# Expert-layer tiles cut along the batches, the left-over rows in short units of 128, and x transposed 128 rows at a time

## The chip, the cores and the metric

The kernel runs on one core of one Trainium2 chip. The metric is the device time of the whole program in microseconds, median of three runs.

## The reference

Decayed causal attention over 8 batches of 8 heads, 576 positions of width 64, and then a two-layer expert block ("moe") on the 4608 rows of 512 values that come out, with 2048 hidden columns. Rows are the positions of a batch, one batch after the other.

```python
# per head of a batch
scores = scale * np.matmul(q, k.transpose(0, 1, 3, 2))
cum = np.cumsum(np.log(np.clip(f, 0.0001, 1.0)), axis=-1)
scores = np.where(causal, -1000000000.0, scores + cum[..., :, None] - cum[..., None, :])
attn = softmax(scores)                     # rows over their sum + 1e-9
x = np.matmul(attn, v)                     # heads side by side: 4608 x 512
# two layers
h = x @ w_in                               # 512 -> 2048
g = h * np.clip(h + 3.0, 0.0, 6.0) / 6.0
out = g @ w_out                            # 2048 -> 512
```

## The kernel before, in words

**Attention.** The heads are worked off one after the other: four pairs "A" and eight heads "B" for batch 0 (in two parts), then 56 whole heads "F" for batches 1 to 7. For an F head, `rows` (from line 591) makes the scores on TensorE in two halves (`pn`, lines 608 and 611), takes the row maxima on VectorE while it copies (`pp`, line 619), the exponentials on ScalarE (631), splits the result into a high and a low half-precision part in `ring` (ScalarE 645, VectorE 648, GpSimd 642, 654 and 659), and transposes that by DMA into `pT` (line 666, two a head). `av` multiplies it with v (`pav`, lines 691 to 696) and divides by the row sums into `xf` and its two halves `xhl`, [128, 5 chunks, 2 halves, 128 columns of a head pair]. In F heads chunk 0 holds the batch's first 64 positions and chunks 1 to 4 hold 128 each; in A and B heads chunks 0 to 3 hold 128 and chunk 4 the last 64.

**v.** `load_v(b)` loads a batch's v into the one buffer `vst` with three DMAs: two small ones (line 359) and the large one (360). `v_split` (lines 396 and 397) turns a head pair's part into half-precision v; `vst` may only be overwritten when the last pair of a batch is split. `v_scale` takes the greatest value of the new v on VectorE (`vm`, line 365) and makes the batch's scale from it.

**x.** When a head pair is done, `x_move` (line 736) transposes `xhl` by DMA into `xT`, from which the first layer reads. SP issues every DMA of the kernel, in the order of its queue.

**Two layers.** The 4608 rows are cut into nine tiles of 512 rows, whatever the batch: tile t holds the last 64 t rows of batch t - 1 and the first 512 - 64 t of batch t, and tiles 7 and 8 both need batch 7. For each of 16 groups of 128 hidden columns `h_unit` (769) makes 12 products of 512 columns into one PSUM bank (`ph`, lines 778 to 780: high x high, high x low, low x high, over four blocks of 128 inputs), ScalarE applies the first half of the activation with the batch's scale, once for each batch in the tile (788), VectorE the second (791), and ScalarE (792) and VectorE (793) split the result into `gT`. `out_unit` (796) then makes 128 rows of output from 48 products of 512 columns (`po`, lines 800 to 802), scales them (811) and stores them (812). Banks come from three buffers in turn.

**What sets the order.** The tiles are generators in a queue (`queue`, `fill`): between the steps of a head, as many product groups are taken from the queue as a rate says. The rate is fixed for batches 0 and 1, and from batch 2 on (`even`) spreads what is queued over the heads of a batch, so that a tile of batch b is worked off during batch b + 1. `done` queues tile b when batch b's x has been moved, and tiles 7 and 8 at the end. Below that, a list scheduler fixes each engine's final order when the program is built, by priorities and its own cost table; on the chip every engine goes through its list in order.

Of the kernel before, what the change touches and what calls it, by code (L numbers as in the profile page):

```python
# [20 lines left out]
def kernel(  # L21
# [23 lines left out]
    NCC = DM // P  # L45
    NFC = DFF // P
    TT = 512
# [70 lines left out]
    def init_qk(i, eng):  # L118
# [14 lines left out]
    w1 = [cpool.tile([P, NCC, DFF], F16, name=f"w1{i}") for i in range(2)]  # L133
    w2 = cpool.tile([P, NFC + 1, 2, DM], F16, name="w2")
    gT = cpool.tile([P, 2, NFC, TT], F16, name="gT")
    xT = [cpool.tile([P, NCC, 2, TT // P, 2, 64], F16, name=f"xT{i}") for i in range(3)]

    v0 = [
        v16.bitcast(F32).rearrange("p n c j e -> p (n c j e)")[:, 0:3 * VR],
        xT[2].bitcast(F32).rearrange("p a h c l t -> p (a h c l t)")[:, 0:2 * VR],  # L140
    ]
    v0 = [t.rearrange("p (c e) -> p c e", e=VR) for t in v0]

# [6 lines left out]
    NG = 4  # L150
# [49 lines left out]
    def scol(c):  # L200
        return SC[:, c:c + 1]
# [534 lines left out]
    def x_move(v):  # L736

        kind, n = VH[v]
        g = n if kind == "A" else n // 2
        b, cc = divmod(g, NPAIR)  # L740
        xhl = xpair[g][1]
        c0, c1 = {"A": (0, CA), "B": (CA, NCH), "F": (0, NCH)}[kind]

        if kind == "F":
            runs = [(0, 0, 1, 0), (0, 1, NCH, 1), (64, 1, NCH, 2)]
        else:
            runs = [(r * 64, c0, min(c1, NCH - r), r + 2 * c0) for r in range(2)]
        for r, c, last, u in runs:
            while c < last:
                t, q = divmod(S // 64 * b + u, TT // 64)  # L750
                k = min(last - c, (TT // 64 - q + 1) // 2)
                nc.sync.dma_start_transpose(  # L752
                    xT[t % 3][:, cc, q % 2, q // 2:q // 2 + k].rearrange("p c a t -> p (c a) t"),
                    xhl[r:r + 64, c:c + k].rearrange("p c a e -> p (c a e)"),
                )
                c += k
                u += 2 * k


    turn = [0]  # L760
# [1 line left out]
    def mm_tile(name, three):  # L762

        turn[0] += 1
        if three and turn[0] % 3 == 0:
            return ps_t.tile([P, TT], F32, tag="tr", name=name)
        return ps_m.tile([P, TT], F32, tag="mm", name=name)

    def h_unit(t, fc, c0, c1):
        x = xT[t % 3]  # L770
        nw = c1 - c0
        ph = mm_tile(f"ph_{t}_{fc}_{c0}", t > 0 or c0 > 0)[:, :nw]
        fs_ = slice(fc * P, (fc + 1) * P)
        for cc in range(NCC):
            xh, xl = (
                x[:, cc, :, c0 // P:c1 // P, hl].rearrange("p h c t -> p c h t") for hl in range(2)
            )
            nc.tensor.matmul(ph, w1[0][:, cc, fs_], xh, start=(cc == 0), stop=False)  # L778
            nc.tensor.matmul(ph, w1[0][:, cc, fs_], xl, start=False, stop=False)  # L779
            nc.tensor.matmul(ph, w1[1][:, cc, fs_], xh, start=False, stop=(cc == NCC - 1))  # L780
            if cc == 1 and nw == TT:
                yield H_COST
        r = p2.tile([P, TT], F32, tag="rt", name=f"r_{t}_{fc}_{c0}", bufs=3)[:, :nw]
        segs = [(0, nw, min(t, B - 1))]
        if 0 < t < B:
            segs = [(0, 64 * t, t - 1), (64 * t, TT, t)]
        for a, e, b in segs:
            nc.scalar.activation(  # L788
                r[:, a:e], ph[:, a:e], AF.Relu, bias=bias_r, scale=scol(A1 + NG * b + fc * NG // NFC)
            )  # L790
        nc.vector.scalar_tensor_tensor(r, r, 6.0 * CG, ph, op0=ALU.min, op1=ALU.mult)  # L791
        nc.scalar.copy(gT[:, 0, fc, c0:c1], r)  # L792
        nc.vector.tensor_tensor(gT[:, 1, fc, c0:c1], r, gT[:, 0, fc, c0:c1], op=ALU.subtract)  # L793
        yield H_COST

    def out_unit(t, s):
        po = mm_tile(f"po_{t}_{s}", t > 0 or s * P >= QA)
# [7 lines left out]
        g = t * 4 + s  # L805
        b = (g * P) // S
        col = UO + b
        if (g * P + P - 1) // S != b:
            col = UX + b + 1
        o = p2.tile([P, DM], F32, tag="o", name=f"o_{t}_{s}")  # L810
        nc.scalar.activation(o, po, AF.Copy, scale=scol(col))
        nc.sync.dma_start(out[g * P:(g + 1) * P, :], o)
        yield 2.0 - H_COST

    def moe_tile(t, c0=0, c1=TT):
        for fc in range(NFC):
            j, new = divmod(fc, NFC // NG)
            if new == 0 and t < B and c0 == 0:
# [7 lines left out]
        if t < B and c0 == 0:  # L826
            moe_scale_out(t)
        for s in range(c0 // P, c1 // P):
            yield from out_unit(t, s)


    dec = decay()
# [48 lines left out]
    def queue(unit, columns):  # L881
        units.append(unit)
        left[0] += TILE * columns / TT
# [22 lines left out]
    def one(*a):  # L906
        yield from moe_tile(*a)

    def done(v):
        kind, n = VH[v]  # L910
        if kind == "A":
            if n == NPAIR - 1:
                queue(one(0, 0, QA), QA)
            return
        b, h = divmod(n, H)
        if h == H - 1:
            queue(one(b, QA if b == 0 else 0, TT), TT - QA if b == 0 else TT)
            if b == B - 1:
                queue(one(B), TT)

    prev = None
    pend_x = moved = None
# [115 lines left out]
```

## Time and profile before

| | |
|---|---|
| runs | 1094.17, 1095.14, 1095.26 us (median 1095.14) |
| profiled execution, first to last instruction | 1093.0 us |
| TensorE busy (products) | 1013.8 us, 93% |
| VectorE, ScalarE, GpSimd busy | 728.9, 609.7, 414.4 us |
| mean granted TensorE clock | 0.981 |
| x transposes on SP (line 752) | 148 |

A row of a group in the profile gives line, engine, operation, what it writes and reads, shapes and count, then the busy time, the mean of one in ns, and the engine's idle time just before these instructions with what ended it. A row of the waits gives the engine and line that waited, what released it, and the total, count and longest wait. A row of the chain or the timeline begins with its start and its duration in us. A q behind an engine's name stands for its sequencer, which waits and issues DMAs. Products overlap, so the pace of a stream of products is read from the difference of their starts.

### The profile page before, as it was taken

How to read it: one execution, taken by the hardware profiler on the slowest of the kernel's cores; microseconds unless marked ns; L12 is line 12 of the kernel's file. 1: busy time of each engine (PE TensorE's matmuls, PEld its weight loads, DVE VectorE, ACT ScalarE, POOL GpSimd, SP SyncE). 2: the span in 40 equal slices, each digit the busy share in tenths (PEclk: the TensorE clock that was granted, in tenths of full speed). 3: DMA queues.
4: the chain of work that ended last, by engine and by line, in shares of the span. 5: the costliest groups of instructions: out<-in, count | busy, mean ns of one | idle time of the engine just before them, and what ended most of it. 6: DMA issues, size and time to landing. Idle time of an engine off the chain costs nothing.

```text
span 1093.0 us, 20322 instructions
## 1 busy us (share of the span) xinstructions
PE 1013.8 (93%) x7074; PEld 576.3 (53%) x7074; DVE 728.9 (67%) x1903; ACT 609.7 (56%) x1285; POOL 414.4 (38%) x505
## 2 busy tenths in 40 slices
PE   2799977899999989998999889999999999999998
PEld 2568844755555545554555445555555554444443
DVE  7888889877887669756876588569856840520520
ACT  4786656756765557545754566458646831621520
POOL 8443465345545434444534335453555300000000
PEclk9999989999999989998999989999999999999999
DMA  8966447866767656566566755785566530000001
GB/s 251 283 196 211 119 101 131 182 139 137 169 136 155 144 138 130 108 145 155 108 121 129 170 105 116 146 185 104 116 136 145 98 77 29 1 5 34 1 1 39
DMA packets 261651, 133.74 MB, mean 122 GB/s; under 512 B 229445, under 2 KB 231037, under 8 KB 261549
## 3 DMA queue, kind: packets, MB, share of 16 engines
q1 hardware_dynamic: 261548, 132.45, 54.0%
q8 instruction: 56, 0.92, 0.4%
q14 instruction: 47, 0.38, 0.1%
HBM read 47.93 MB, written 9.73 MB: 53 GB/s over the span
## 4 chain that ended last, share of the span: by engine, by line
PE 59%; DMA 6%; DVE 4%; issue 3%; SPq 3%; ACT 3%; POOL 2%; POOLq 0%; DVEq 0%; ACTq 0%
PE po L800 9%; PE po L802 9%; PE po L801 9%; PE ph L778 8%; PE ph L779 8%; PE ph L780 8%; DMA pT<-ring 3%; PE pn L611 3%; PE pn L608 3%; DMA vst<-in_vS_dram 2%; SPq L752 2%; DVE pp L619 1%; ACT pp L631 1%; PE pav L695 1%; PE pav L696 1%
## 5 line engine op out<-in xcount | busy, mean ns | idle before, releaser
L778 PE MATMUL ph<-xT,w 128*128 128x512 f16 (+1 forms) x640 | 229.2, 364 | 19.6 <-DVE r L791 19.4
L779 PE MATMUL ph<-xT,w 128*128 128x512 f16 (+1 forms) x640 | 228.5, 363 | 0.0
L780 PE MATMUL ph<-xT,w 128*128 128x512 f16 (+1 forms) x640 | 228.2, 362 | 0.0
L801 PE MATMUL po<-w,gT 128*128 128x512 f16 x576 | 214.3, 381 | 7.3 <-DVE w L294 7.3
L800 PE MATMUL po<-w,gT 128*128 128x512 f16 x576 | 212.1, 381 | 3.0 <-ACT w L283 2.2
L802 PE MATMUL po<-w,gT 128*128 128x512 f16 x576 | 214.1, 381 | 0.0
L631 ACT ACTIVATE pp<-pp,nb 128x192 f32<-128x192 f32 x280 | 138.8, 553 | 128.2 <-DVE nb L625 127.9
L648 DVE TENSOR_TENSOR ring<-pp,ring 128x128 f16<-128x128 f32 (+2 forms) x216 | 135.0, 635 | 70.1 <-ACT ring L645 69.2
L791 DVE SCALAR_TENSOR_TENSOR r<-r,ph 128x512 f32<-128x512 f32 (+1 forms) x160 | 99.9, 626 | 104.6 <-ACT r L788 104.4
L788 ACT ACTIVATE r<-ph,bias_r,SC 128x256 f32<-128x256 f32 (+7 forms) x272 | 144.1, 571 | 37.2 <-PE ph L780 33.3
L458 POOL TENSOR_TENSOR T<-ST,T 64x576 fp32r<-64x576 f32 (+1 forms) x68 | 100.6, 1480 | 153.5 <-DMA T<-TK 149.6
L792 ACT CAST gT<-r 128x512 f16<-128x512 f32 (+1 forms) x160 | 91.9, 575 | 89.6 <-DVE r L791 89.5
L619 DVE CUSTOM_DVE_ANT_0 pp<-pn,W 128x192 f32<-128x192 f32 x280 | 123.3, 482 | 26.1 <-PE pn L611 19.8
L608 PE MATMUL pn<-TK,TQ 68*128 68x192 f32 x336 | 127.0, 390 | 5.6 <-issue 4.0
L793 DVE TENSOR_TENSOR gT<-r,gT 128x512 f16<-128x512 f32 (+1 forms) x160 | 110.4, 693 | 29.2 <-ACT gT L792 28.5
L611 PE MATMUL pn<-T,T 128*128 128x192 f32 x336 | 116.2, 375 | 0.4 <-POOL T L458 0.4
L645 ACT CAST ring<-pp 128x192 f16<-128x192 f32 x280 | 115.7, 452 | 0.0
L455 POOL TENSOR_TENSOR T<-ST,TQ 64x576 fp32r<-64x576 f32 (+2 forms) x68 | 96.8, 1423 | 18.4 <-PE pn L611 8.7
L779 PEld LDWEIGHTS <-w 128*128 128x128 f16 x640 | 63.1, 99 | 75.2 <-issue 26.2
L780 PEld LDWEIGHTS <-w 128*128 128x128 f16 x640 | 63.2, 99 | 65.8 <-issue 9.2
L802 PEld LDWEIGHTS <-gT 128*128 128x128 f16 x576 | 56.5, 98 | 76.0 <-issue 14.6
L778 PEld LDWEIGHTS <-w 128*128 128x128 f16 x640 | 62.4, 99 | 59.1 <-issue 10.8
(136 smaller groups left out, 1713.6 us busy)
## 6 DMA issues: line engine op xcount, KB each, us to landing
ST<-in_qk_dram SPq DMA_DIRECT2D x64, 288.0 KB
T<-TK SPq DMA_DIRECT2D x64, 144.0 KB
out_dram<-o SPq DMA_DIRECT2D x36, 256.0 KB
ring<-in_w_out_dram SPq DMA_DIRECT2D x16, 512.0 KB
T<-TQ SPq DMA_DIRECT2D x56, 144.0 KB
vst<-in_vS_dram SPq DMA_DIRECT2D x7, 1040.0 KB
ring<-in_w_in_dram SPq DMA_DIRECT2D x9, 512.0 KB
w<-in_w_in_dram SPq DMA_DIRECT2D x7, 512.0 KB
```

The source lines that it names most:

```text
L608: nc.tensor.matmul(dst, TQ[i][0:D + 4, qs], TK[i][0:D + 4, a:e], start=True, stop=False)
L611: nc.tensor.matmul(dst, T7[j][:, qs], T1[j][:, a:e], start=False, stop=True)
L619: nc.vector.tensor_tensor_reduce(pp[:r, w:w + kw], pn[:r, o:o + kw], W[:r, 4 * P + r - kw:4 * P + r], 1.0, -3.0e38, ALU.add, ALU.max, accu ...
L631: nc.scalar.activation(x_, x_, AF.Exp, bias=nb[:r, e0 + x:e0 + x + 1], scale=0.125)
L648: eng.tensor_tensor(hl[:r, a:a + c * P], pp[:r, at[c] + 64:at[c] + kw], hl[:r, h0[c] + 64:h0[c] + kw], op=ALU.subtract,)
L778: nc.tensor.matmul(ph, w1[0][:, cc, fs_], xh, start=(cc == 0), stop=False)
L779: nc.tensor.matmul(ph, w1[0][:, cc, fs_], xl, start=False, stop=False)
L780: nc.tensor.matmul(ph, w1[1][:, cc, fs_], xh, start=False, stop=(cc == NCC - 1))
L788: nc.scalar.activation(r[:, a:e], ph[:, a:e], AF.Relu, bias=bias_r, scale=scol(A1 + NG * b + fc * NG // NFC))
L800: nc.tensor.matmul(po, gT[:, 0, fc, ts_], w2[:, fc, 0, :], start=(fc == 0), stop=False)
L801: nc.tensor.matmul(po, gT[:, 0, fc, ts_], w2[:, fc, 1, :], start=False, stop=False)
L802: nc.tensor.matmul(po, gT[:, 1, fc, ts_], w2[:, fc, 0, :], start=False, stop=(fc == NFC - 1))
```

## The change

- Tile t now holds 512 rows of batch t alone: the first 512 of batch 0, the last 512 of the other batches. There are eight such tiles, and each is one batch's, so line 788 runs once for a bank.
- The other 64 rows of each batch go to a second, small buffer `xS`. Those of two batches form a short tile of 128 rows, queued (`moe_short`) behind the tile of every odd batch. `h_short` makes four groups of 128 hidden columns in one bank, [128, 4, 128 rows], each by 12 products of 128 columns; the bank is then worked off like a whole one, with one ScalarE pass for each of the two batches. One `out_unit` follows; its 128 rows are stored as two times 64, but for the first pair.
- `x_move` transposes all 128 rows of the chunks at once into `xT` (one DMA), and the 64-row chunk into `xS` (another), where it issued four or five DMAs of 64 rows for a late pair. `xT` has two buffers in place of three.

The diff, cut to what matters:

```diff
-    xT = [cpool.tile([P, NCC, 2, TT // P, 2, 64], F16, name=f"xT{i}") for i in range(3)]
+    xT = [cpool.tile([P, NCC, TT // P, 2, P], F16, name=f"xT{i}") for i in range(2)]
+    xS = [cpool.tile([P, NCC, 2, 2, 64], F16, name=f"xS{i}") for i in range(2)]
...
-        if kind == "F":
-            runs = [(0, 0, 1, 0), (0, 1, NCH, 1), (64, 1, NCH, 2)]
-        else:
-            runs = [(r * 64, c0, min(c1, NCH - r), r + 2 * c0) for r in range(2)]
-        for r, c, last, u in runs:
-            while c < last:
-                t, q = divmod(S // 64 * b + u, TT // 64)
-                k = min(last - c, (TT // 64 - q + 1) // 2)
-                nc.sync.dma_start_transpose(
-                    xT[t % 3][:, cc, q % 2, q // 2:q // 2 + k].rearrange("p c a t -> p (c a) t"),
-                    xhl[r:r + 64, c:c + k].rearrange("p c a e -> p (c a e)"),
-                )
...
+        full, short = {"A": ((0, CA), None), "B": ((CA, 4), 4), "F": ((1, NCH), 0)}[kind]
+        d0 = full[0] - (kind == "F")
+        n = full[1] - full[0]
+        nc.sync.dma_start_transpose(
+            xT[b % 2][:, cc, d0:d0 + n].rearrange("p c a t -> p (c a) t"),
+            xhl[:, full[0]:full[1]].rearrange("p c a e -> p (c a e)"),
+        )
+        if short is not None:
+            nc.sync.dma_start_transpose(
+                xS[b // 2 % 2][:, cc, b % 2],
+                xhl[0:64, short].rearrange("p a e -> p (a e)"),
+            )
...
-        segs = [(0, nw, min(t, B - 1))]
-        if 0 < t < B:
-            segs = [(0, 64 * t, t - 1), (64 * t, TT, t)]
-        for a, e, b in segs:
-            nc.scalar.activation(
-                r[:, a:e], ph[:, a:e], AF.Relu, bias=bias_r, scale=scol(A1 + NG * b + fc * NG // NFC)
-            )
+        nc.scalar.activation(
+            r, ph, AF.Relu, bias=bias_r, scale=scol(A1 + NG * t + fc * NG // NFC)
+        )
...
+    def h_short(u, j):
+        x = xS[u % 2]
+        n = NFC // NG
+        ph = mm_tile(f"phs_{u}_{j}", True).rearrange("p (f t) -> p f t", f=n)
+        for i in range(n):
+            fs_ = slice((n * j + i) * P, (n * j + i + 1) * P)
+            for cc in range(NCC):
+                xh, xl = (x[:, cc, :, hl] for hl in range(2))
+                nc.tensor.matmul(ph[:, i], w1[0][:, cc, fs_], xh, start=(cc == 0), stop=False)
+                nc.tensor.matmul(ph[:, i], w1[0][:, cc, fs_], xl, start=False, stop=False)
+                nc.tensor.matmul(ph[:, i], w1[1][:, cc, fs_], xh, start=False, stop=(cc == NCC - 1))
+            if i == 1:
+                yield H_COST
...
+        for h in range(2):
+            nc.scalar.activation(
+                r[:, :, 64 * h:64 * h + 64], ph[:, :, 64 * h:64 * h + 64], AF.Relu, bias=bias_r,
+                scale=scol(A1 + NG * (2 * u + h) + j),
+            )
...
+    def moe_short(u):
+        for j in range(NG):
+            yield from h_short(u, j)
+        a, b = 2 * u, 2 * u + 1
+        yield from out_unit(0, True, UX + b, [b * S - 64] if a == 0 else [a * S, b * S])
...
-            if b == B - 1:
-                queue(one(B), TT)
+            if b % 2:
+                queue(moe_short(b // 2), P)
```

**What moves on the engines.** In the new kernel's order the line numbers are higher by one up to `x_move`: the loads of v are 360 and 361, pT 667, T 454 and 455, vm 366; the x transposes are 748 (128 rows) and 753 (64 rows), the short unit's products 797 to 799, the store 828.

SP's queue at the border from batch 5 to batch 6, where v of batch 6 is loaded, before:

```order
L812 DMA out_dram<-o_3_7300 128x512
L752 DMA_TRANSPOSE xT_119<-xhl_7131 128x2x64 x2
L752 DMA_TRANSPOSE xT_117<-xhl_7131 128x6x64
L752 DMA_TRANSPOSE xT_119<-xhl_7131 128x2x64
L752 DMA_TRANSPOSE xT_117<-xhl_7131 128x6x64
L666 DMA_TRANSPOSE pT_7310<-ring_124 128x13x128
L417 DMA TK_98<-decay_dram 2x576
L419 DMA TQ_95<-decay_dram 2x576
L666 DMA_TRANSPOSE pT_7310<-ring_125 128x12x128
L453 DMA T_102<-TQ_94 64x576
L454 DMA T_100<-TK_97 64x576
L360 DMA vst<-in_vS_dram 128x4x520
```

The two small loads of v (359) stand just ahead of the first of these rows. The same place now:

```order
L667 DMA_TRANSPOSE pT_7565<-ring_126 128x13x128
L667 DMA_TRANSPOSE pT_7565<-ring_124 128x12x128
L412 DMA ST_103<-in_qk_dram 128x576
L360 DMA vst<-in_vS_dram 64x520 x2
L361 DMA vst<-in_vS_dram 128x4x520
L748 DMA_TRANSPOSE xT_118<-xhl_7532 128x8x128
L753 DMA_TRANSPOSE xS_119<-xhl_7532 128x2x64
L667 DMA_TRANSPOSE pT_7752<-ring_125 128x13x128
L828 DMA out_dram<-o_7741 64x512 x2
```

The large load of v has moved ahead of the x transposes and directly behind the small ones; a load of the next head's q and k (ST) stands ahead of all three. At the borders to batches 5 and 7 the two x transposes of the pair stand between the small loads and the large one.

VectorE's order at the same border, around vm, before:

```order
L791 SCALAR_TENSOR_TENSOR r_3_0_7483<-r_3_0_7483,ph_3_0_7424 128x512
L625 TENSOR_SCALAR nb_7493<-MF_108 128x3
L793 TENSOR_TENSOR gT<-r_3_0_7483,gT 128x512
L619 ISA pp_1_7551,MF_108<-pn_1_7546,W 128x320
L619 ISA MF_108 128x1
L619 ISA pp_1_7551,MF_108<-pn_1_7546,W 128x448
L619 ISA MF_108 128x1
L365 TENSOR_REDUCE vm_8048<-vst 128x1 x2
L625 TENSOR_SCALAR nb_7493<-MF_108 128x2
L791 SCALAR_TENSOR_TENSOR r_4_0_7531<-r_4_0_7531,ph_4_0_7518 128x512
```

The same place now:

```order
L620 ISA pp_0_7763,MF_109<-pn_0_7754,W 64x64
L620 ISA MF_109 64x1
L727 TENSOR_TENSOR xf_7531<-pav,rs_1_7729 128x5x64
L626 TENSOR_SCALAR nb_7753<-MF_109 128x3
L733 TENSOR_TENSOR xhl_7532<-xf_7531,xhl_7532 128x5x128
L784 SCALAR_TENSOR_TENSOR r_0_0_7791<-r_0_0_7791,ph_0_0_7778 128x512
L649 TENSOR_TENSOR ring_125<-pp_0_7763,ring_125 128x128
L649 TENSOR_TENSOR ring_125<-pp_0_7763,ring_125 128x512
L366 TENSOR_REDUCE vm_8469<-vst 128x1 x2
L786 TENSOR_TENSOR gT<-r_0_0_7791,gT 128x512
L620 ISA pp_1_7817,MF_109<-pn_1_7812,W 128x320
```

vm has moved forward by about one and a half heads: it stands behind the first half of a head's row maxima, and the last reader of the old v (`L398`, the split of batch 5's last pair) is the fourteenth row ahead of it, where in the old order it stood two heads ahead.

More of the change, by code (lines that the diff above doesn't have):

```diff
@@ L135 @@
     gT = cpool.tile([P, 2, NFC, TT], F16, name="gT")
-    xT = [cpool.tile([P, NCC, 2, TT // P, 2, 64], F16, name=f"xT{i}") for i in range(3)]
+    xT = [cpool.tile([P, NCC, TT // P, 2, P], F16, name=f"xT{i}") for i in range(2)]
+    xS = [cpool.tile([P, NCC, 2, 2, 64], F16, name=f"xS{i}") for i in range(2)]
     v0 = [
         v16.bitcast(F32).rearrange("p n c j e -> p (n c j e)")[:, 0:3 * VR],
-        xT[2].bitcast(F32).rearrange("p a h c l t -> p (a h c l t)")[:, 0:2 * VR],
+        xT[1].bitcast(F32).rearrange("p a c l t -> p (a c l t)")[:, 0:2 * VR],
     ]
@@ L742, in x_move @@
         c0, c1 = {"A": (0, CA), "B": (CA, NCH), "F": (0, NCH)}[kind]
-        if kind == "F":
-            runs = [(0, 0, 1, 0), (0, 1, NCH, 1), (64, 1, NCH, 2)]
-        else:
-            runs = [(r * 64, c0, min(c1, NCH - r), r + 2 * c0) for r in range(2)]
-        for r, c, last, u in runs:
-            while c < last:
-                t, q = divmod(S // 64 * b + u, TT // 64)
-                k = min(last - c, (TT // 64 - q + 1) // 2)
-                nc.sync.dma_start_transpose(
-                    xT[t % 3][:, cc, q % 2, q // 2:q // 2 + k].rearrange("p c a t -> p (c a) t"),
-                    xhl[r:r + 64, c:c + k].rearrange("p c a e -> p (c a e)"),
-                )
-                c += k
-                u += 2 * k
+        full, short = {"A": ((0, CA), None), "B": ((CA, 4), 4), "F": ((1, NCH), 0)}[kind]
[10 more added lines that the diff above has]
+            )
     turn = [0]
@@ L769, in h_unit @@
     def h_unit(t, fc, c0, c1):
-        x = xT[t % 3]
+        x = xT[t % 2]
         nw = c1 - c0
@@ L774, in h_unit @@
         for cc in range(NCC):
-            xh, xl = (
-                x[:, cc, :, c0 // P:c1 // P, hl].rearrange("p h c t -> p c h t") for hl in range(2)
-            )
+            xh, xl = (x[:, cc, c0 // P:c1 // P, hl] for hl in range(2))
             nc.tensor.matmul(ph, w1[0][:, cc, fs_], xh, start=(cc == 0), stop=False)
@@ L783, in h_unit @@
         r = p2.tile([P, TT], F32, tag="rt", name=f"r_{t}_{fc}_{c0}", bufs=3)[:, :nw]
-        segs = [(0, nw, min(t, B - 1))]
-        if 0 < t < B:
-            segs = [(0, 64 * t, t - 1), (64 * t, TT, t)]
-        for a, e, b in segs:
-            nc.scalar.activation(
-                r[:, a:e], ph[:, a:e], AF.Relu, bias=bias_r, scale=scol(A1 + NG * b + fc * NG // NFC)
-            )
+        nc.scalar.activation(
+            r, ph, AF.Relu, bias=bias_r, scale=scol(A1 + NG * t + fc * NG // NFC)
+        )
         nc.vector.scalar_tensor_tensor(r, r, 6.0 * CG, ph, op0=ALU.min, op1=ALU.mult)
@@ L794, in h_unit, with out_unit @@
         yield H_COST
-    def out_unit(t, s):
-        po = mm_tile(f"po_{t}_{s}", t > 0 or s * P >= QA)
+    def h_short(u, j):
[11 more added lines that the diff above has]
+                yield H_COST
+        r = p2.tile([P, TT], F32, tag="rt", name=f"rs_{u}_{j}", bufs=3)
+        r = r.rearrange("p (f t) -> p f t", f=n)
+        for h in range(2):
[3 more added lines that the diff above has]
+            )
+        nc.vector.scalar_tensor_tensor(r, r, 6.0 * CG, ph, op0=ALU.min, op1=ALU.mult)
+        g = [gT[:, i, n * j:n * j + n, 0:P] for i in range(2)]
+        nc.scalar.copy(g[0], r)
+        nc.vector.tensor_tensor(g[1], r, g[0], op=ALU.subtract)
+        yield H_COST
+    def out_unit(s, three, col, rows_):
+        po = mm_tile(f"po_{rows_[0]}", three)
         ts_ = slice(s * P, (s + 1) * P)
@@ L804, in out_unit @@
                 yield 2.0 - H_COST
[L805 to L810, printed above, removed]
+        o = p2.tile([P, DM], F32, tag="o", name=f"o_{rows_[0]}")
         nc.scalar.activation(o, po, AF.Copy, scale=scol(col))
-        nc.sync.dma_start(out[g * P:(g + 1) * P, :], o)
+        w = P // len(rows_)
+        for i, r0 in enumerate(rows_):
+            nc.sync.dma_start(out[r0:r0 + w, :], o[i * w:(i + 1) * w])
         yield 2.0 - H_COST
@@ L817, in moe_tile @@
             j, new = divmod(fc, NFC // NG)
-            if new == 0 and t < B and c0 == 0:
+            if new == 0 and c0 == 0:
                 while j not in w_in_done:
@@ L825, in moe_tile @@
                 pass
-        if t < B and c0 == 0:
+        if c0 == 0:
             moe_scale_out(t)
+        r0 = t * S + (64 if t else 0)
         for s in range(c0 // P, c1 // P):
-            yield from out_unit(t, s)
+            yield from out_unit(s, t > 0 or s * P >= QA, UO + t, [r0 + s * P])
+    def moe_short(u):
[3 more added lines that the diff above has]
+        yield from out_unit(0, True, UX + b, [b * S - 64] if a == 0 else [a * S, b * S])
     dec = decay()
```

## The prediction

> **What bounds the kernel now.** I read the page's head first, then busy time by stage, then the waits, then one batch boundary in the chain of waits and in the timeline, and last the durations by shape.
>
> ```profile
> span 1093.0 us, 20322 instructions
> PE 1013.8 (93%) x7074; PEld 576.3 (53%) x7074; DVE 728.9 (67%) x1903; ACT 609.7 (56%) x1285; POOL 414.4 (38%) x505
> ```
>
> The profiled execution took 1093.0 us from first to last instruction. The median of the runs is 1095.14, so 2.1 us lie outside the span; I add them at the end. TensorE is busy for 93% of it. The stages, with duration, then PE busy, PEld, DVE, ACT, POOL, granted clock:
>
> ```profile
> 0.00:200.00 200.00, 153.17 (x1100) 112.52 (x1101) 168.79 (x490) 132.75 (x278) 102.45 (x118) 0.97 0.69 186
> 200.00:400.00 200.00, 188.43 (x1507) 112.19 (x1504) 152.25 (x412) 122.28 (x271) 95.61 (x117) 0.98 0.71 151
> 400.00:650.00 250.00, 234.50 (x1720) 129.88 (x1720) 185.71 (x467) 147.91 (x320) 109.86 (x138) 0.96 0.61 128
> 650.00:900.00 250.00, 249.10 (x1882) 136.51 (x1881) 178.09 (x472) 151.07 (x327) 106.50 (x132) 1.00 0.62 125
> 900.00:1093.00 193.00, 188.58 (x874) 85.23 (x871) 44.05 (x64) 55.74 (x91) 0.00 (x0) 1.00 0.05 16
> ```
>
> TensorE idles 46.8 us in the first 200 us (weights being prepared), 11.6 us in 200 to 400, 15.5 us in 400 to 650, and next to nothing until the 4.4 us of the last output. So from 200 us on it is the bound. Moving expert work from the tail into the batches gains nothing where TensorE is full; what can be gained is the 27 us of idle time between 200 and 650, and the slow clock beside it. Who causes it:
>
> ```profile
> DVE vm L365 <- DMA vst<-in_vS_dram: 26.7, 6, 9.3
> PE ph L778 <- DVE r L791: 19.4, 6, 7.8
> PE pav L691 <- DMA pT<-ring: 9.5, 13, 1.9
> SPq L411 <- POOL T L458: 114.2, 48, 6.0
> ```
>
> VectorE waits 26.7 us at six places for the next batch's v to land, and TensorE waits 19.4 us at six places for VectorE's r, the longest 7.8 us. That the one makes the other is seen in the chain of waits around 620 us:
>
> ```profile
> 610.62 1.22 SPq L752
> 611.89 1.26 SPq L752
> 613.20 2.12 SPq L752
> 615.36 1.26 SPq L752
> 616.79 1.47 SPq L666
> ...
> 622.05 0.59 SPq L454
> 622.69 5.50 DMA vst<-in_vS_dram
> 628.31 0.24 DVE vm L365
> 631.97 0.60 DVE r L791
> 632.62 0.59 PE ph L778
> ```
>
> SP issues x transposes (L752) one after another, then pT (L666), small loads and T (L454), and only then v's last load. It lands after 5.5 us; vm (L365) stands in VectorE's order ahead of r, so r is late, no PSUM bank comes free, and TensorE stops:
>
> ```profile
> 624.67 0.19 PE L696 MATMUL pav<-v,pT 128*128 128x65 f16 x1
> 632.62 0.59 PE L778 MATMUL ph<-xT,w 128*128 128x512 f16 x1 [7.76 <-DVE r L791]
> 633.00 0.63 PE L779 MATMUL ph<-xT,w 128*128 128x512 f16 x1
> 633.42 0.63 PE L780 MATMUL ph<-xT,w 128*128 128x512 f16 x1
> ```
>
> After the stop the products start 0.43 us apart, twice the 0.215 us seen below: the clock is halved for a while, and the granted clock of this stage is 0.96.
>
> **The change, part by part.** *Products.* These rows give the pace of a product with its own weight load, for 512, 256 and 65 columns, by the difference of the starts, and the duration of a weight load:
>
> ```profile
> 1005.38 0.38 PE L778 MATMUL ph<-xT,w 128*128 128x512 f16 x1
> 1005.60 0.38 PE L779 MATMUL ph<-xT,w 128*128 128x512 f16 x1
> 208.04 0.27 PE L779 MATMUL ph<-xT,w 128*128 128x256 f16 x1
> 208.15 0.27 PE L780 MATMUL ph<-xT,w 128*128 128x256 f16 x1
> 893.92 0.19 PE L694 MATMUL pav<-v,pT 128*128 128x65 f16 x1
> 893.95 0.19 PE L695 MATMUL pav<-v,pT 128*128 128x64 f16 x1
> L779 PEld LDWEIGHTS <-w 128*128 128x128 f16 x640 | 63.1, 99 | 75.2 <-issue 26.2
> ```
>
> That is 0.216, 0.11 and 0.03 us, about 0.42 ns a column with 2 ns on top, so I take 0.056 us for 128 columns. The ninth tile's 192 products of 512 columns (192 x 0.216 = 41.4 us) become four short units of 192 products of 128 columns, 768 x 0.056 = 43.0 us: **+1.6 us**. The ends of this price are 0.03 (23 us, a gain of 18) and 0.11 (84.5 us, a loss of 43), and the line through three widths speaks for the middle. The second product keeps its 36 groups of 48.
>
> The Trainium skill, "TensorE: Matmul & The Clock Gate", section "Back-to-back issue gap", says that in a stream of load and product pairs 128 columns sustain about 81 ns each, more than the 56 ns of a lone one. By that the term would be an estimated 62.2 - 41.4 = +20.8 us. The trace speaks against a pace set by the load: 65 columns, each with its own load, go every 0.03 us.
>
> *Evacuation.* A short unit fills one bank with four groups of 128 columns, so VectorE and the second ACT pass keep their count and size. The first ACT pass loses its split at batch borders:
>
> ```profile
> L788 ACT ACTIVATE r<-ph,bias_r,SC 128x256 f32<-128x256 f32 (+7 forms) x272 | 144.1, 571 | 37.2 <-PE ph L780 33.3
> L788 ACT ACTIVATE r<-ph,bias_r,SC 128x256 f32<-128x256 f32 x64 | 34.1, 559 | 11.2 <-PE ph L780 7.6 <-DVE vm L371 2.8 <-DVE nb L625 0.9
> L788 ACT ACTIVATE r<-ph,bias_r,SC 128x512 f32<-128x512 f32 x16 | 12.4, 777 | 9.9 <-PE ph L780 9.9
> ```
>
> It becomes 64 halves at 0.559 and 112 whole banks at 0.777 us, 122.8 us in place of 144.1. ACT is busy for 56% of the span, so I cost these 21 us at nothing; if ACT were late at a bank, it would be a gain.
>
> *Transposes on SP.* Issue times, least, median and most:
>
> ```profile
> L752 SPq DMA_TRANSPOSE xT<-xhl x148: 1160/1245/2385, 47.8 to 899.3; - x148
> L666 SPq DMA_TRANSPOSE pT<-ring x112: 1274/1498/3233, 151.5 to 885.0; - x112
> ```
>
> The 148 transposes become 68. A transpose of 128 rows in eight blocks has no row; L666, 128 rows in 12 or 13 blocks, takes 1.5 us and L752, 64 rows in two to six, 1.245. I take 1.4 for the long and 1.25 for the short, so a late pair costs SP 2.65 us in place of 5 x 1.245 = 6.2. Three stores of output come on top. Over the kernel SP loses 148 x 1.245 = 184 us and gets 36 x 1.4 + 32 x 1.25 = 90.
>
> *What the order makes of it.* In the new order v's last load follows the first two directly at the borders to batches 3, 4 and 6, and after two transposes at those to 5 and 7. That removes what stood ahead of it in the chain (L752 to L454, 12 us). But vm, too, stands earlier on VectorE: at the border to batch 6 it comes 14 rows behind the last reader of the old v (L398), for which the loads must wait. From that reader v needs two small loads and the last one (0.59 us to issue one, by L454's like row, so 1.7), then 5.5 us: 7.2 us.
>
> ```profile
> L619 DVE CUSTOM_DVE_ANT_0 pp<-pn,W 128x192 f32<-128x192 f32 x280 | 123.3, 482 | 26.1 <-PE pn L611 19.8
> L648 DVE TENSOR_TENSOR ring<-pp,ring 128x128 f16<-128x128 f32 (+2 forms) x216 | 135.0, 635 | 70.1 <-ACT ring L645 69.2
> ```
>
> VectorE's rows up to vm are some ten real operations of 0.48 to 0.64 us, 5 to 6 us, plus the wait for ACT's exponentials ahead of L648. So it arrives 1 to 2 us early rather than 4.5 us (26.7 / 6), and TensorE, which had 19.4 / 6 = 3.2 us a border, waits about 1 us: 6 us in all, **-13 us** (ends: 0 and -19.4). Three long stops no longer halve the clock; the six products shown from 632.62 to 634.70 lost 6 x 0.215 = 1.3 us a stop: **-4 us** (ends 0 and -6). The 9.5 us of waits for pT lose a third, since pT queues behind two transposes, not five: **-3 us** (ends +3 and -9.5).
>
> *Tail.* After the last attention product the order holds 756 products, 192 of them short, in place of 900. The 62 us that leave the tail go between attention products where TensorE is full: 0. The last x is covered as before: in both orders 132 output products of tile 6, 28 us, are left when the last attention product is done.
>
> The sum is 1.6 - 13 - 4 - 3 = -18.4, so 1093.0 - 18.4 = 1074.6, and with the 2.1 us outside the span **1077 us**.
>
> **The rivals.** *The stop only moves.* SP's waits for POOL (114.2 us in 48, up to 6.0) stay, and the load of ST stands right ahead of v's; gains at the borders are eaten by other late inputs, T and pT among them. Left is -3 to +3 us: 1092 to 1098. For it: VectorE idles for many releasers. Against: TensorE was full from 650 to 900 with the same releasers.
>
> *Slower: v is tied too closely to its reader.* With vm 14 rows behind the reader, 7.2 us of loading and up to 6.0 us of SP waiting stand against 5 us of cover, and VectorE stops for up to 8 us at each of six borders. It decides once TensorE's stops exceed 19.4 - 1.6 = 17.8 us in all, 3.0 us a border, with clock and pT as before. At 6 us a border it costs 36 - 19.4 + 1.6 = 18.2 us and 4 us of slow clock at three more long stops, 1117 us; at 4.5 us and half that clock about 1106. Against it: the exponentials ahead of L648 give cover.
>
> *Slower: each short product waits for its weight load*, 0.099 us by the row: 76.0 - 41.4 = +34.6 in place of +1.6, 1110 us. The point from which it decides is (41.4 + 20) / 768 = 0.080 us. The row of 0.03 us speaks clearly against it. The skill's 81 ns would land at that point, by estimate 1096 us.
>
> **How the numbers follow.** Forecast 0.68; the stop only moves 0.14; v too close 0.13; weight load 0.05. Faster by more than 0.2% (2.2 us, about what a measurement can tell): the forecast and a third of the second, 0.73. Same: 0.07. Slower: 0.20. The likeliest case is 1077. Its low end takes every gain at its better end, 1.6 - 19.4 - 6 - 9.5 = -33.3, 1062; I stop at 1063. The high end takes in the case of the moved stop, 1098; the two slower cases stay mostly outside.
>
> **What would show it.** In the new profile: short products every 0.056 us; 68 x transposes; the waits of vm for v well below 26.7 us and those of ph for r below 10; granted clock near 1.00 from 400 to 650 and under 6 us of idle TensorE there; the tail after the last attention product near 133 us. The forecast is wrong if vm still waits over 4 us a border, if short products are 0.08 us or more apart, or if TensorE's idle time turns up before other inputs.

## The result, and the profile after

| | before | after |
|---|---|---|
| median of the runs | 1095.2 us (1094.17 to 1096.66) | 1079.26 us (1076.71 to 1081.78) |
| ratio, 95% interval | | 0.9851 [0.9827, 0.9876] |
| profiled execution | 1093.0 us | 1076.4 us |
| mean granted clock | 0.981 | 0.989 |

The change makes the kernel faster by 1.5%. The profile's head and the busy time by stage of the changed kernel, in the columns of the prediction's stage table (duration, then PE, PEld, DVE, ACT, POOL, then granted clock):

```profile
span 1076.4 us, 21155 instructions
PE 1012.2 (94%) x7650; PEld 600.5 (56%) x7650; DVE 731.5 (68%) x1903; ACT 587.9 (55%) x1189; POOL 407.8 (38%) x505
```

```profile
0.00:200.00 200.00, 156.82 (x1069) 114.75 (x1070) 174.70 (x489) 132.34 (x277) 106.48 (x121) 0.96 0.71 189
200.00:400.00 200.00, 194.02 (x1645) 119.95 (x1644) 150.81 (x401) 116.23 (x247) 85.62 (x108) 0.99 0.69 143
400.00:650.00 250.00, 248.90 (x1985) 142.01 (x1984) 178.82 (x460) 143.21 (x290) 105.95 (x135) 1.00 0.60 126
650.00:900.00 250.00, 247.79 (x1948) 140.82 (x1947) 178.71 (x458) 144.42 (x291) 106.16 (x137) 1.00 0.61 123
900.00:1076.40 176.40, 164.70 (x1013) 82.97 (x1011) 48.44 (x99) 51.74 (x88) 3.61 (x6) 0.99 0.12 29
```

TensorE's busy time is nearly what it was (1013.8 and 1012.2 us): the gain is idle time. By stage it idles 43.2, 6.0, 1.1, 2.2 and 11.7 us, where it idled 46.8, 11.6, 15.5, 0.9 and 4.4. So 14.4 us came from 400 to 650, 5.6 from 200 to 400, 3.6 from the start, while 1.3 us were given back from 650 to 900 and 7.3 at the end. The clock of 400 to 650 went from 0.96 to 1.00. The waits that answer to those of before (total, count, longest):

```profile
DVE vm L366 <- DMA vst<-in_vS_dram: 7.1, 6, 2.6
PE ph L775 <- DVE r L784: 6.9, 8, 1.7
PE pav L692 <- DMA pT<-ring: 5.0, 4, 2.2
PE phs L797 <- DVE rs L809: 3.3, 1, 3.3
```

VectorE's waits for v fell from 26.7 to 7.1 us and TensorE's for r from 19.4 to 6.9, the longest from 7.8 to 1.7. The last row is new, and belongs to the tail. SP's queue and VectorE at the border to batch 6, where TensorE stopped for 7.76 us before:

```profile
622.19 1.02 SPq L412 DMA_DIRECT2D ST<-in_qk_dram  x1
623.53 1.95 SPq L360 DMA_DIRECT2D vst<-in_vS_dram  x2
625.53 0.58 SPq L361 DMA_DIRECT2D vst<-in_vS_dram  x1
626.70 1.31 SPq L748 DMA_TRANSPOSE xT<-xhl  x1
628.06 1.24 SPq L753 DMA_TRANSPOSE xS<-xhl  x1
```

```profile
622.96 0.54 DVE L398 SCALAR_TENSOR_TENSOR v<-vst,SC,v 128x320 f16<-128x320 f32 x1
631.43 2.88 DVE L366 TENSOR_REDUCE vm<-vst 128x1 f32<-128x1536 f32 x2 [2.15 <-DMA vst<-in_vS_dram]
```

The last reader of the old v (L398) ends at 623.50, the small loads go at 623.53 and the large one at 625.53, ahead of the two x transposes. vm starts at 631.43, 7.9 us behind the reader, of which VectorE waited 2.15 for v; of the 5.8 us before that, it worked 4.0 and waited 1.8 for ScalarE. TensorE does not stop there.

The end of the program is where time was lost. TensorE in the last short unit, and ScalarE beside it:

```profile
1051.60 0.33 PE L799 MATMUL phs<-xS,w 128*128 128x128 f16 x3
1055.21 0.22 PE L797 MATMUL phs<-xS,w 128*128 128x128 f16 x1 [3.28 <-DVE rs L809]
...
1068.31 0.39 PE L819 MATMUL po<-w,gT 128*128 128x512 f16 x1 [2.49 <-ACT gT L811]
```

```profile
1051.92 2.84 ACT L805 ACTIVATE rs<-phs,bias_r,SC 128x256 f32<-128x256 f32 x6 [6.58 <-PE phs L799]
```

The products of three short banks end together at 1051.9, and ScalarE gets six passes at once after 6.58 us without work. The fourth group of products finds no free PSUM bank until VectorE has read the first (3.28 us), and the output products wait for the last gT (2.49 us).

### The profile page after: what moved, and what is told of

It is laid out like the page before. It is cut to its first block, busy times and chain, and to the rows that moved or that the text cites. A ratio compares the mean times of both kernels' runs of the same rounds, so it can differ in the third digit from the quotient of the medians.

```text
span 1076.4 us, 21155 instructions
## 1 busy us (share of the span) xinstructions
PE 1012.2 (94%) x7650; PEld 600.5 (56%) x7650; DVE 731.5 (68%) x1903; ACT 587.9 (55%) x1189; POOL 407.8 (38%) x505
## 4 chain that ended last, share of the span: by engine, by line
PE 65%; DVE 17%; ACT 6%; issue 5%; DMA 5%; SPq 1%; POOL 1%; ACTq 0%; DVEq 0%; POOLq 0%
PE po L819 10%; PE po L821 10%; PE po L820 10%; PE ph L775 7%; PE ph L776 6%; PE ph L777 6%; DVE pp L620 3%; PE pn L609 3%; PE pn L612 3%; ACT pp L632 2%; DVE ring L649 2%; DMA vst<-in_vS_dram 2%; DVE gT L786 2%; DVE r L784 1%; DVE nb L626 1%
## 5 line engine op out<-in xcount | busy, mean ns | idle before, releaser
L775 PE MATMUL ph<-xT,w 128*128 128x512 f16 (+1 forms) x576 | 200.2, 358 | 7.1 <-DVE r L784 6.9
L649 DVE TENSOR_TENSOR ring<-pp,ring 128x128 f16<-128x128 f32 (+2 forms) x216 | 144.5, 678 | 83.6 <-ACT ring L646 80.8
L776 PE MATMUL ph<-xT,w 128*128 128x512 f16 (+1 forms) x576 | 199.7, 357 | 0.0
L777 PE MATMUL ph<-xT,w 128*128 128x512 f16 (+1 forms) x576 | 199.2, 357 | 0.0
L447 POOL TENSOR_SCALAR TK<-ST 64x576 fp32r<-64x576 f32 (+1 forms) x68 | 50.1, 737 | 245.2 <-PE pn L609 202.5
L784 DVE SCALAR_TENSOR_TENSOR r<-r,ph 128x512 f32<-128x512 f32 (+1 forms) x144 | 89.1, 620 | 54.6 <-ACT r L781 54.2
L785 ACT CAST gT<-r 128x512 f16<-128x512 f32 (+1 forms) x144 | 81.5, 569 | 76.9 <-DVE r L784 76.2
L786 DVE TENSOR_TENSOR gT<-r,gT 128x512 f16<-128x512 f32 (+1 forms) x144 | 102.8, 717 | 20.6 <-ACT gT L785 19.0
L781 ACT ACTIVATE r<-ph,bias_r,SC 128x512 f32<-128x512 f32 (+1 forms) x144 | 103.6, 724 | 20.7 <-PE ph L777 17.5
L456 POOL TENSOR_TENSOR T<-ST,TQ 64x576 fp32r<-64x576 f32 (+2 forms) x68 | 100.2, 1474 | 14.2 <-PE pn L612 5.3
L821 PEld LDWEIGHTS <-gT 128*128 128x128 f16 x576 | 56.5, 99 | 71.1 <-issue 9.4
L820 PEld LDWEIGHTS <-gT 128*128 128x128 f16 x576 | 56.5, 99 | 63.4 <-issue 6.4
L655 POOL TENSOR_TENSOR ring<-pp,ring 128x128 f16<-128x128 f32 x96 | 59.9, 624 | 78.2 <-ACT ring L646 33.9
```

The lines of the kernel that those rows point to most:

```text
L649: eng.tensor_tensor(hl[:r, a:a + c * P], pp[:r, at[c] + 64:at[c] + kw], hl[:r, h0[c] + 64:h0[c] + kw], op=ALU.subtract,)
```

## The experiments

Two theories stood against each other. *Theory 1*, the prediction's: what was removed is the wait for v at the batch borders, with the slow clock behind it. *Theory 2*: the new balance (short work between attention, one pass for a bank) is worth the time, or SP's relief as a whole (T and pT too) and not v. And the given-back time of the tail had to be explained. Each run's ratio is to the kernel before on the same chip.

### v's load first, in the kernel before

```diff
-            load_v(b + 1)
+            with tc.high_priority():
+                load_v(b + 1)
```

> The kernel before with one edit: v's three loads are traced at high priority, so that the large one stands directly behind the small ones on SP, ahead of the x transposes. Tiles, short rows and transposes are as before. Theory 'v's stop' (the gain of the change comes from v landing before VectorE asks for it): 1077 to 1084 us, the waits of vm for v fall from 26.7 us to under 10 and TensorE's idle time from 400 to 650 from 15.5 to under 5 us. Rival 'balance' (the gain comes from 62 us of expert work that leave the tail for idle stretches of TensorE between attention products): 1095 us, no change. Rival 'fewer passes' (the gain comes from ScalarE's whole-bank passes): 1095 us.

Measured: **1090.68 us**, ratio 0.9941 [0.9921, 0.9961], two fifths of the gain (0.59% of 1.49%). The large load now stood directly behind the small ones on SP, but the scheduler also moved vm forward:

```profile
DVE vm L365 <- DMA vst<-in_vS_dram: 20.5, 5, 7.0
PE ph L778 <- DVE r L791: 16.1, 7, 4.8
```

```profile
605.05 1.14 SPq L359 DMA_DIRECT2D vst<-in_vS_dram  x2
606.24 0.58 SPq L360 DMA_DIRECT2D vst<-in_vS_dram  x1
```

```profile
598.63 0.76 DVE L397 SCALAR_TENSOR_TENSOR v<-vst,SC,v 128x320 f16<-128x320 f32 x1
613.07 2.88 DVE L365 TENSOR_REDUCE vm<-vst 128x1 f32<-128x1536 f32 x2 [6.81 <-DMA vst<-in_vS_dram]
```

No x transpose stands ahead of v's large load any more, and still VectorE stands 6.81 us. The last reader of the old v (L397) ends at 599.39 us, but SP, with transposes of pT and loads of T and ST ahead, comes to the loads only at 605.05, 5.7 us later (4.5 and 2.2 at the borders to batches 4 and 5), where in the changed kernel it is 0.03 us. From there v takes 8.0 us to land. And vm now comes as soon as 6.9 us behind the reader, about as in the changed kernel (5.8). This is the prediction's rival "v is tied too closely to its reader", with the waiting of SP that it names. The run decided between the theories only in so far as moving the load is not enough while SP comes late; the wait itself stayed.

### The wait for v taken away, on the old tiles

To take the wait away, vm must keep its distance. Here v's loads again stand ahead of the x transposes, and vm is ordered behind the last row maxima of the batch's last head, three heads later. The 148 transposes on SP and the old tiles stay.

```diff
-            load_v(b + 1)
+            with tc.high_priority():
+                load_v(b + 1)
...
+            with tc.issue_after(latest[0]) if b > 1 else nullcontext():
                 nc.vector.tensor_reduce(
...
-        if b + 1 < B and h == 7:
-            vq = v_scale(b + 1)
         next(vq, None)
...
         if b + 1 < B and h == 7:
+            vq = v_scale(b + 1)
             for _ in vq:
```

`latest` holds the last instruction of line 619.

> The kernel before (148 x transposes on SP, old tiles) with v's loads ahead, as in the run with v first (1090.68 us), and with vm put three heads later in VectorE's order, behind the last row maxima of the batch's last head. So nothing waits for v any more, and all else on SP is as before. Theory 1 (v's wait alone made the stops, as the prediction had it): VectorE's waits for v under 3 us, TensorE's stops for r under 7 us, and the gain of 13 to 17 us comes, 1077 to 1083 us. Theory 2 (SP's queue as a whole is the cause, and the transposes make T and pT late as well): waits for v gone, but only part of the gain, 1085 to 1091. Third case (v's split now comes late and TensorE waits for v): 1092 to 1100.

Measured: **1079.98 us**, ratio 0.9835 [0.9810, 0.9860]. The waits:

```profile
PE ph L782 <- DVE r L795: 1.4, 3, 0.6
DVE vm L368 <- DMA vst<-in_vS_dram: 0.5, 1, 0.5
PE pav L695 <- DMA pT<-ring: 19.0, 21, 3.0
```

The waits for v and for r are nearly gone, those for pT are twice as long as before (9.5 us), and a gain as large as the change's is there, with all 148 transposes still on SP. So taking v's wait away is enough for it, as Theory 1 has it. The gain of 17.5 us (1097.47 us on the same chip, and 1079.98) is near the 17 that the prediction gave to the stops and the clock together, but it isn't the same sum: by the profiles, TensorE waits 18.0 us less for r and 9.5 more for pT, and idles 5.4 us less in the first 200 us (41.4 and 46.8), which no term of the prediction covers.

### x transposes in more pieces, in the changed kernel

The 128-row transpose is cut into two of 64 rows (three DMAs a late pair), or into four of 64 rows and two chunks (five). Over the kernel these are 104 and 160 transposes, beside 68 in the changed kernel and 148 before.

```diff
+        for r in range(0, P, 64):
+            for c in range(0, n, 4):          # 2 for five a pair
+                e = min(c + 4, n)
                 nc.sync.dma_start_transpose(
-                    xT[b % 2][:, cc, d0:d0 + n]...
+                    xT[b % 2][:, cc, d0 + c:d0 + e, :, r:r + 64]...
```

> The changed kernel, with the 128-row transpose cut into two of 64 rows: three DMAs for a late pair, between the two of the changed kernel (1079 us) and the five of the run with pieces (1095 us). If the cost is SP's issue time for each DMA (1.24 us by the trace), it is a third of the way: 1083 to 1086 us. If it is only v's load behind five of them at two borders: 1079 to 1081 us. If 64-row transposes are slow in themselves, however many: 1090 us or more.

> The changed kernel, with x transposed in pieces of 64 rows and at most two chunks again: four DMAs and the short one for a late pair, five in place of two, as many as before the change. Theory 'v's stop': at three of five borders v's load still stands ahead of the x transposes, at two it stands behind five of them; so one or two stops return and the time is 1081 to 1087 us. 'Balance' and 'fewer passes': 1079 us, as the changed kernel.

Measured: **1088.26 us** with three, ratio 0.9915 [0.9883, 0.9948], and **1094.95 us** with five, 0.9982 [0.9957, 1.0006]. With 1079.26 for two, the gain shrinks with three and is gone with five, although tiles, short units and passes are all new. With three, then with five:

```profile
DVE vm L366 <- DMA vst<-in_vS_dram: 12.3, 6, 5.3
```

```profile
DVE vm L366 <- DMA vst<-in_vS_dram: 14.8, 6, 4.1
PE ph L778 <- DVE r L787: 12.6, 13, 3.1
```

The waits for v come back in part (7.1, 12.3, 14.8 us). They do not hold all of it: with five, TensorE waits 5.7 us more for r (12.6 and 6.9), and the kernel takes 16 us more. The two longest of these stops, 2.65 and 3.06 us, come behind the waits for v at the borders to batches 5 and 7. At the first of them the small loads of v go at 506.9 us and the large one at 521.0, with five x transposes, two of pT and four small loads in between: so far the theory of v's stop held. The stages of that run:

```profile
0.00:200.00 200.00, 154.33 (x1055) 113.38 (x1056) 165.86 (x486) 130.43 (x274) 99.99 (x118) 0.95 0.67 182
200.00:400.00 200.00, 193.95 (x1637) 120.23 (x1634) 150.34 (x395) 116.72 (x249) 84.55 (x105) 0.98 0.67 144
400.00:650.00 250.00, 245.18 (x1926) 138.89 (x1925) 172.44 (x446) 136.82 (x277) 103.45 (x134) 0.99 0.60 127
650.00:900.00 250.00, 243.93 (x1923) 138.30 (x1922) 178.32 (x450) 141.33 (x286) 109.16 (x136) 1.00 0.57 120
900.00:1093.00 193.00, 179.88 (x1120) 91.40 (x1118) 63.34 (x129) 62.11 (x107) 10.30 (x14) 0.99 0.17 36
```

Against the changed kernel that is 2.5, 0.1, 3.7, 3.9 and 1.4 us more idle time, 11.6, and 5 us more busy time (1017.3 and 1012.2) under a clock lower by 0.01 in three stages. So the loss is spread over four of the five stages; one row doesn't hold it. Part of it is the start: there TensorE waits 2.7 us for the second layer's weights in the changed kernel, and 10.3 and 9.6 us with three and five transposes a pair (9.5 before). That the gain is gone with five doesn't mean that v's stop is back in full, either: r costs 12.6 us there and not 19.4, and the two stops of the tail and the 1.5 us of products are paid as in the changed kernel.

The runs show that cutting the x transposes on SP into more pieces takes the gain away. They don't separate the number of the pieces from their size: 1088.26 lies between the 1083 to 1086 us expected of the issue time and the 1090 of transposes that are slow in themselves, and each edit also gives SP a new order.

### x transposes on another engine's queue

Issue time on SP could be relieved without any new tiling, by issuing the x transposes from ScalarE: in the kernel before, in the one with five pieces, and in the one with short banks in turn (below). The edit is the same in all three:

```diff
-                nc.sync.dma_start_transpose(
+                nc.scalar.dma_start_transpose(
```

> The kernel before, with nothing changed but that its 148 x transposes are issued on ScalarE's queue and not on SP's. Theory (the gain is issue time on SP, some 1.25 us a transpose, with v, T and pT behind it): most of the gain comes without the new tiling, 1076 to 1084 us, VectorE's waits for v under 10 us in all. Rival 1 (the many small transfers themselves slow the other transfers down, whoever issues them): 1091 to 1096. Rival 2 (the issues cost ScalarE as much as they cost SP, and its exponentials and activation passes come late): 1095 to 1110.

> The kernel after with the x transposes in five pieces a late pair (1094.95 us with the pieces on SP), the pieces issued on ScalarE's queue. Theory (issue time on SP): the loss of the pieces goes, 1076 to 1083 us. Rival 1 (the small transfers themselves): 1092 to 1097. Rival 2 (ScalarE late by the issues): 1090 to 1110.

> The kernel after with short banks in turn (1071.81 us), its 68 x transposes issued on ScalarE's queue. Theory (issue time on SP): what is left of the waits for v (5.5 us) and for pT (9 us) goes in part, 1066 to 1071 us. Rival 1 (transfers) and a third case, that two transposes a pair are already beside other work: 1071 to 1073. Rival 2 (ScalarE late by some 85 us of issues): 1074 to 1085.

Measured: **1171.06 us**, ratio 1.0674 [1.0641, 1.0707]; **1182.65 us**, 1.0797 [1.0768, 1.0827]; **1105.43 us**, 1.0082 [1.0056, 1.0107]. All far slower, by about half a microsecond for each transpose moved: (1171.06 - 1097.2) / 148 = 0.50 (1097.2 is the kernel before on the same chip), (1182.65 - 1094.95) / 160 = 0.55, (1105.43 - 1071.81) / 68 = 0.49. In the first of the three v's wait did shrink (in the third it grew, from 5.5 to 14.2 us), and ScalarE became late. The last row is of SP's queue:

```profile
DVE vm L365 <- DMA vst<-in_vS_dram: 10.9, 5, 5.5
ACT ring L645 <- issue: 42.2, 9, 9.7
ACT gT L792 <- issue: 35.7, 8, 7.5
PE ph L778 <- DVE r L791: 43.1, 13, 9.2
SPq L666 <- DMA xT<-xhl: 137.8, 44, 8.8
```

```profile
612.07 2.50 ACTq L752 DMA_TRANSPOSE xT<-xhl  x2
614.61 0.62 ACT L792 CAST gT<-r 128x512 f16<-128x512 f32 x1 [5.88 <-issue]
```

A gT cast that stands behind two transposes waits 5.88 us, and VectorE's r and TensorE's ph after it. Only 2.50 us of that is the issue of the two: ScalarE's pass before ends at 608.73 us, and the transposes go at 612.07. So Rival 2 of the expectations, with its price set too low, is one part. The other is in the last row of the waits, which has no like in the kernel before: SP's transposes of pT wait 137.8 us at 44 places until x transposes issued by ScalarE have landed (142.6 us at 42 and 60.8 at 18 in the other two runs). The Trainium skill, "DMA: Bandwidth & Descriptors", section "Silent corruption: two transposing streams in flight at once", says that transposes issued from one of the two engines have to wait until those of the other have landed. The waits on SP agree with that. None of the expectations had this case, and no run separates its price from that of the issue on ScalarE. SP was not relieved, so these three runs say that ScalarE is no place for the x transposes while SP issues those of pT, and little about the issue time on SP.

### ScalarE's passes

The single pass of a bank is cut in two again, at the column where it was cut before: once in the changed kernel, once with short banks in turn.

```diff
-        nc.scalar.activation(r, ph, AF.Relu, ...)
+        cut = 64 * t if 0 < t else nw
+        for a, e in ((0, cut), (cut, nw)):
+            if a < e:
+                nc.scalar.activation(r[:, a:e], ph[:, a:e], AF.Relu, ...)
```

> The changed kernel, with the first ScalarE pass over each whole bank cut in two at 64 t columns again, 112 passes more. 'Fewer passes': most of the 16 us gain is lost, 1088 to 1095 us. 'v's stop' and 'balance': ScalarE has room, 1078 to 1081 us.

> The same as the run with the banks in turn, and the first ScalarE pass over each whole bank cut in two again (112 passes more), so that the tail is alike in both. If passes cost nothing: the same time within 2 us. If they matter once the tail is equal: 4 to 7 us slower than the run with the banks in turn.

Measured: **1077.61 us**, ratio 0.9825 [0.9792, 0.9858], and **1074.43 us**, 0.9774 [0.9741, 0.9807], beside 1079.26 and 1071.81 without the second pass. Both pairs of intervals overlap, so no cost of the passes is measured, and 'fewer passes' as the source of the gain is out. The second run is 2.6 us above its partner, between the two cases of its expectation: a cost of a few us can't be excluded.

### The tail: place or order

The last short unit is queued ahead of the last tile, so that it is not the program's end:

```diff
+            if b == B - 1:
+                queue(moe_short_first(b // 2), P)
...
-            if b % 2:
+            if b % 2 and b < B - 1:
```

`moe_short_first` makes the batch's scales, then calls `moe_short`.

> The changed kernel, with the last short unit queued ahead of the last whole tile instead of behind it. In the changed kernel's tail TensorE stops for 3.3 us because three banks of short products end together and for 2.5 us ahead of the last output products. If these two stops come from the short unit being last, they are hidden by the whole tile and the time falls by 4 to 6 us to 1073 to 1075 us. If they are the short unit's own (its banks always end together), it stays at 1079.

Measured: **1076.66 us**, ratio 0.9821 [0.9791, 0.9852], the same as the changed kernel within the intervals. The first stop moved with the unit:

```profile
972.63 0.22 PE L797 MATMUL phs<-xS,w 128*128 128x128 f16 x1 [2.75 <-DVE rs L809]
```

TensorE's wait ahead of the unit's output products shrank to 0.6 us, but at 989.51 it stops for another 2.05 us, for r. So a new place hides little. Next, the order: the scheduler had mixed the products of three short banks. Here each bank's products are held behind the last product of the bank before, and the output's behind the last bank:

```diff
+    behind = []
...
+            with tc.issue_after(behind[-1]) if j else nullcontext():
                 for cc in range(NCC):
...
-                    nc.tensor.matmul(ph[:, i], w1[1][:, cc, fs_], xh, ...)
+                    m = nc.tensor.matmul(ph[:, i], w1[1][:, cc, fs_], xh, ...)
...
+        behind.append(m.ins)
```

> The changed kernel, with the four banks of a short unit held in turn on TensorE: each bank's products are queued behind the bank before it and the unit's output products behind the last bank. In the changed kernel's tail the scheduler has interleaved three banks, and TensorE stops for 3.3 and 2.5 us. If the interleaving makes these stops, both go and the time falls by 5 to 7 us, to 1072 to 1075 us. If four groups in a bank are the cause, whatever their order, the stops stay and so does 1079.

Measured: **1071.81 us**, ratio 0.9765 [0.9737, 0.9794], faster than both kernels; its interval lies below that of the changed kernel. ScalarE in its last short unit:

```profile
1043.35 1.02 ACT L809 ACTIVATE rs<-phs,bias_r,SC 128x256 f32<-128x256 f32 x2 [1.61 <-PE phs L802]
...
1048.71 1.02 ACT L809 ACTIVATE rs<-phs,bias_r,SC 128x256 f32<-128x256 f32 x2 [0.29 <-PE phs L802]
...
1051.39 1.02 ACT L809 ACTIVATE rs<-phs,bias_r,SC 128x256 f32<-128x256 f32 x2 [0.29 <-PE phs L802]
```

Of the four banks the first, third and fourth are shown: one is ready every 2.68 us (48 products at 0.056), and each is worked off while the next is filled. TensorE no longer waits there.

### The balance

All four short units are put at the end, with four buffers `xS` and banks in turn, so that no short work lies between attention products:

```diff
-            if b % 2:
-                queue(moe_short(b // 2), P)
+            if b == B - 1:
+                for u in range(B // 2):
+                    queue(moe_short(u), P)
```

> The same as the run with the banks in turn, with all four short units queued at the end behind the last whole tile (four small x buffers), so that three short units, 62 us of products, go back from batches 2, 4 and 6 into the tail. 'Balance' as the gain: the batches keep idle stretches that the units filled, and the time rises by 8 us or more. 'SP' as the gain: TensorE is full in the batches, so they shorten by what the tail grows, and the time is within 4 us of the run with the banks in turn.

Measured: **1075.25 us**, ratio 0.9793 [0.9762, 0.9824], beside 1071.81: the intervals overlap and the medians are 3.4 us apart, within the 4 us of 'SP' and not the 8 or more of 'balance'. With the passes, this takes the first half of Theory 2 away as the main source of the gain.

## Why the prediction was right, point by point

**The sum.** 1077.0 was forecast and 1079.26 measured; the profiled span fell by 16.6 us where 18.4 were worked out. The main mechanism, the stops behind v, was right. That the number came out so near is partly luck: the tail (+7.3 us) was set at nothing, and against it stood 3.6 us at the start, which no term covers, and a larger gain on pT than was put down.

**Products, +1.6: right.** The short products start 0.056 us apart:

```profile
1048.92 0.22 PE L799 MATMUL phs<-xS,w 128*128 128x128 f16 x1
...
1049.59 0.22 PE L799 MATMUL phs<-xS,w 128*128 128x128 f16 x1
```

These are twelve steps in 0.67 us, and 768 of them make 42.9 us, +1.5. The line through three widths held. The 81 ns that the Trainium skill, "TensorE: Matmul & The Clock Gate", section "Back-to-back issue gap", gives for 128 columns are not seen here: the measured 56 ns decide, each product with its own weight load.

**Evacuation, 0: right** by the two runs with the second pass.

**Transposes on SP: right in kind, a little high.** There are 68, and the long one is no dearer than the short one (least, median, most):

```profile
L748 SPq DMA_TRANSPOSE xT<-xhl x36: 1198/1232/1982, 50.2 to 934.2; - x36
```

```profile
L753 SPq DMA_TRANSPOSE xS<-xhl x32: 1157/1234/2062, 102.3 to 935.5; - x32
```

They take 36 x 1.232 + 32 x 1.234 = 83.8 us where 90 were estimated; 1.4 us for the long one, taken between two rows, was too much.

**The order, -13 and -4: right, and shown.** At the border to batch 6 the prediction had 7.2 us from the reader to v's arrival and 5 to 6 us of cover; the trace has 7.9 and 5.8, and 2.15 us of wait where 1 to 2 were expected. Over the kernel TensorE's waits for r fell by 12.5 us. Two readings were loose, though. The prediction shared the 19.4 us among six borders; in the kernel before 18.0 of them are at three, behind the three longest waits for v, one in the prediction's rows and these two:

```profile
402.26 0.59 PE L778 MATMUL ph<-xT,w 128*128 128x512 f16 x1 [5.18 <-DVE r L791]
516.08 0.59 PE L778 MATMUL ph<-xT,w 128*128 128x512 f16 x1 [5.03 <-DVE r L791]
```

And the 6 us that were to be left came out as 6.9, but not behind v: of the eight waits for r in the changed kernel only one, of 1.2 us, follows a wait for v. So v's stops went almost whole, and the closeness of 6 and 6.9 is chance.

What the prediction put down to the order alone depends on more: with the order's edit by itself (v first) only two fifths came, since SP reached the loads 2.2 to 5.7 us behind the reader, and with three or five transposes a pair in the new kernel the gain shrank to about half and to nothing.

**pT, -3: right in direction, too small.** TensorE's products waited 5.0 us for pT in place of 9.5. Of the 5.0, 4.1 are in the first 200 us (1.6 before); behind them the wait fell from 7.9 to 0.9.

**The tail, 0: wrong, and the step that failed.** The prediction counted 756 products behind the last attention product and made it about 133 us. From that product to the end:

```profile
931.40 0.19 PE L697 MATMUL pav<-v,pT 128*128 128x65 f16 x1
...
1070.99 0.38 PE L821 MATMUL po<-w,gT 128*128 128x512 f16 x1
```

That is 139.6 us. The prediction counted products and not who frees their banks: a short bank takes 2.7 us of products as an h bank of 12 long ones takes 2.6, but the scheduler filled three at once, and then nothing was left to hide six ScalarE passes. With the banks in turn the same stretch takes 133.2:

```profile
928.13 0.19 PE L697 MATMUL pav<-v,pT 128*128 128x65 f16 x1
...
1061.33 0.38 PE L826 MATMUL po<-w,gT 128*128 128x512 f16 x1
```

So the count itself was right, 133.2 us against about 133. Behind the last product 1.4 us more passed as well: 5.0 us from its end to the end of the span, and 3.6 before.

**What the sum left out.** TensorE idles 3.6 us less in the first 200 us. Its waits for the second layer's weights fell there from 9.5 to 2.7 us, while others grew; no run tried that by itself. By stage, idle time changed by -3.6 us in the start, -18.7 from 200 to 900 us (r -11.9 and pT -7.0 account for it) and +7.3 in the last stage, -15.0 together. With +1.5 for the products, some 3 us of the 16.6 are left for the clock, which was put at 4; that remainder is worked out, not measured.

**The rivals.** "The stop only moves" did not happen. "v is tied too closely to its reader" did not happen in the changed kernel, whose longest wait for v is 2.6 us, but it is what the run with v first shows, at three borders with waits of 4 to 7 us; so it had been right to keep a price on it. "Each short product waits for its weight load" fell with the 0.056 us.

**What stays open.** Why the pieces lose time in nearly every stage, and not only where v waits (the wait for r holds 5.7 of 16 us); whether their number or their size does it; and what moved the start, where the run without the wait for v, with 148 transposes, gained 5.4 us too.

## What to carry to other kernels

A load that is late is judged by two distances, what stands ahead of it on its queue and how far its reader stands behind it on the engine: moving the load alone also moved the reader forward, while the queue still came to the load late, and only two fifths of the gain came; moving the reader back as well brought all of it. Where one queue issues everything, count what a load has to stand behind: here two, three and five transposes a pair gave 1079, 1088 and 1095 us. Pushing them to an engine that also computes cost much more than it could save, on that engine and, by the transposes that waited for each other, on the first queue. When work is cut into short units, count what has to be read out of the PSUM banks as well as the products, and look whether the scheduler fills several banks at once.

## What the runs showed of the hardware that was not expected

- A DMA transpose of 128 rows in eight blocks holds SP for 1.232 us (median), one of 64 rows in two blocks for 1.234: between these two the price was by the DMA, not by its size. With 12 or 13 blocks it was 1.498 (the prediction's row of line 666).
- A product of 128 columns with its own weight load went every 0.056 us, while the rows give a weight load 0.099 us: loads overlap.
- A transpose issued by ScalarE holds its queue for 1.207 us (median of 148; 1.245 on SP before), not longer than on SP, and yet each one cost the kernel about 0.5 us; SP's own transposes then waited 137.8 us for those of ScalarE to land.
